# Scores and the carried-state product of a chunked retention kernel as pairs of 64x64 array tiles, in place of zero-padded 128x128 operands

## The chip, the cores and the metric

The kernel runs on one core of one Trainium2 chip. The metric is the device time of one execution in microseconds (us); the profiled span is 1 to 2 us shorter than that time. PE is TensorE's matmul row in the profile and PEld its weight loads; DVE is VectorE, ACT is ScalarE, POOL is GpSimd.

## The reference, cut to what matters

```python
# q, k, v: [8 batches, 8 heads, 576 tokens, 64]; gamma by head; pos = token index
scores = (q @ k.T) / sqrt(64)                        # per batch and head
ret    = scores * where(rel >= 0, gamma ** rel, 0)   # rel = pos_query - pos_key
attn   = ret @ v
x      = attn as [8*576 tokens, 8*64 features]
h      = x @ w_in                                    # 512 -> 2048
out    = maximum(0.01 * h, h) @ w_out                # 2048 -> 512
```

The kernel splits the sequence into chunks of 64 tokens. Inside a chunk it computes masked scores times v; what earlier chunks contribute comes from a carried 64x64 state per head. Two heads are stacked on the 128 partitions (`NP` = 4 such pairs), and a *unit* is up to two chunks (128 tokens) of one batch: 40 units, of which 8 have one chunk only. The two dense layers then run in token blocks, and the attention of later units is threaded between their matmuls.

## The kernel before

Two heads share the 128 rows of the array, and their products must not mix. So the stationary operand is made block diagonal: a 128x128 tile, zeroed once, of which only the two diagonal 64x64 blocks are rewritten. Three tiles of that sort matter: `kdiag` (scores), `sdiag` (carried product) and `vdiag` (product inside the chunk). Writing the two diagonal blocks takes two half-height writes.

```python
# st_transpose(u): tr is PSUM, [P, (q,k), NP, P]
nc.scalar.copy(out=qT[:, :, 0:n], in_=tr[:, 0, :, 0:n])
for hh in range(2):
    eng = nc.scalar.copy if (hh == 0 or u < 2) else nc.vector.tensor_copy
    eng(out=kdiags[z][CH*hh : CH*hh+CH, :, 0:nb, CH*hh : CH*hh+CH], in_=tr[CH*hh : CH*hh+CH, 1, ...])
# st_state(u, j): ut accumulates k^T v in PSUM over three chunks
nc.tensor.matmul(out=ut[:, p, :], lhsT=kstks[z][:, p, j, :], rhs=vst[u][:, p, j, :], ...)
for hh in range(2):
    dst = sd[lo:hi, :, lo:hi]                         # sd is an sdiag
    ...                                               # copy of the state, or ut + sins, by DVE (one of the first by ACT)
# st_scores(u): per p and chunk j
nc.tensor.matmul(out=sc[:, p, j, :], lhsT=kdiags[z][:, p, j, :], rhs=qTs[u][:, p, CH*j : CH*j+CH], ...)
# st_out(u): per chunk j and p, alternating
nc.tensor.matmul(out=o, lhsT=vdiags[z][:, p, j, :], rhs=s16s[u][:, p, j, :], start=True, stop=(i == 0))
if i > 0:
    nc.tensor.matmul(out=o, lhsT=sdiag_at[b, i][:, p, :], rhs=qTs[u][:, p, CH*j : CH*j+CH], start=False, stop=True)
...   # (cuts: loads, casts, dense layers, schedule)
```

Of the kernel before, what the change touches and what calls it, by code (L numbers as in the profile page):

```python
# [11 lines left out]
F16 = mybir.dt.float16  # L12
MUL = mybir.AluOpType.mult
ADD = mybir.AluOpType.add
# [4 lines left out]
def kernel(  # L19
# [16 lines left out]
    nc = tc.nc  # L36
# [3 lines left out]
    P = 128  # L40
    CH = 64
    BLK = 3 * CH
    NP = H // 2
# [9 lines left out]
    for w in range(3):  # L53
        r = ((P * w + np.arange(P)) % BLK)[:, None] - BLK / 2
# [12 lines left out]
    const_pool = ctx.enter_context(tc.tile_pool(name="const", bufs=1))  # L67
    ld_pool = ctx.enter_context(tc.tile_pool(name="ld", bufs=4))
    a_pool = ctx.enter_context(tc.tile_pool(name="ap", bufs=4))
# [22 lines left out]
    w_out16 = const_pool.tile([P, NF, DM], F16, name="w_out16")  # L92

    NZ = 2
    kdiags = [const_pool.tile([P, NP, 2, P], F16, name=f"kdiag{z}") for z in range(NZ)]
    kstks = [const_pool.tile([P, NP, 2, P], F16, name=f"kstk{z}") for z in range(NZ)]
    vdiags = [const_pool.tile([P, NP, 2, P], F16, name=f"vdiag{z}") for z in range(NZ)]
    NS = 3
    sdiags = [const_pool.tile([P, NP, P], F16, name=f"sdiag{z}") for z in range(NS)]
    halves = [const_pool.tile([P, H, D], F16, name=f"half{x}") for x in range(2)]  # L100

    units = [(b, w) for b in range(B) for w in range((S + P - 1) // P)]
# [52 lines left out]
        nc.scalar.copy(out=t[:, :, 0:nb, :], in_=v32[u][:, :, 0:nb, :])  # L155

    qTs = {}
    s16s = {}
    ups = {}
    sins = {}  # L160
    scount = [0]
    sdiag_at = {}

    def st_transpose(u):
        b, w = units[u]
        n = nrows[u]
        nb = n // CH
        z = u % NZ
        for hh in range(2):
            nc.vector.tensor_copy(  # L170
                out=vdiags[z][CH * hh : CH * hh + CH, :, 0:nb, CH * hh : CH * hh + CH],
                in_=vst[u][CH * hh : CH * hh + CH, :, 0:nb, :],
            )
        k16 = qk16[u, 1].rearrange("s (p h) d -> s p h d", h=2)
        if not (w == 4):
            for j in range(nb):
                for hh in range(2):
                    (nc.scalar.copy if u < 4 else nc.gpsimd.tensor_copy)(  # L178
                        out=kstks[z][CH * hh : CH * hh + CH, :, j, CH * hh : CH * hh + CH],
                        in_=k16[CH * j : CH * j + CH, :, hh, :],  # L180
                    )
        tr = tr_pool.tile([P, 2, NP, P], F16, name="tr")
        for x in range(2):
            for p in range(NP):
                nc.tensor.transpose(  # L185
                    tr[:, x, p, :],
                    qk16[u, x][:, 2 * p : 2 * p + 2, :].rearrange("t h d -> t (h d)"),
                    ident,
                )
        qT = a_pool.tile([P, NP, P], F16, name="qT")  # L190
        qTs[u] = qT
        nc.scalar.copy(out=qT[:, :, 0:n], in_=tr[:, 0, :, 0:n])  # L192
        for hh in range(2):
            eng = nc.scalar.copy if (hh == 0 or u < 2) else nc.vector.tensor_copy
            eng(  # L195
                out=kdiags[z][CH * hh : CH * hh + CH, :, 0:nb, CH * hh : CH * hh + CH],
                in_=tr[CH * hh : CH * hh + CH, 1, :, 0:n].rearrange(
                    "e p (j c) -> e p j c", c=CH
                ),
            )  # L200

    def st_state(u, j):
        b, w = units[u]
        z = u % NZ
        i = 2 * w + j
        if i == NI - 1:
            return
        if i % 3 == 0:
            ups[b] = u_pool.tile([P, NP, CH], FP, name="ups")
        ut = ups[b]  # L210
        for p in range(NP):
            nc.tensor.matmul(  # L212
                out=ut[:, p, :],
                lhsT=kstks[z][:, p, j, :],
                rhs=vst[u][:, p, j, :],
                start=(i % 3 == 0 and p == 0),
                stop=(i % 3 == 2),
                skip_group_check=True,
            )
        nxt = i + 1  # L220
        sd = sdiags[scount[0] % NS]
        scount[0] += 1
        sdiag_at[b, nxt] = sd
        if nxt % 3 == 0:
            new = a_pool.tile([P, NP, CH], FP, name="sinit")
            gb = gblk_sb.unsqueeze(2).to_broadcast([P, NP, CH])
            if nxt == 3:
                nc.vector.tensor_tensor(out=new, in0=ut, in1=gb, op=MUL)
            else:
                tmp = a_pool.tile([P, NP, CH], FP, name="stmp")  # L230
                nc.vector.tensor_tensor(out=tmp, in0=ut, in1=sins[b], op=ADD)
                nc.vector.tensor_tensor(out=new, in0=tmp, in1=gb, op=MUL)
            sins[b] = new
        for hh in range(2):
            lo, hi = CH * hh, CH * hh + CH
            dst = sd[lo:hi, :, lo:hi]
            if nxt % 3 == 0:
                nc.vector.tensor_copy(out=dst, in_=sins[b][lo:hi])
            elif nxt < 3:
                (nc.scalar.copy if hh == 0 else nc.vector.tensor_copy)(out=dst, in_=ut[lo:hi])  # L240
            else:
                nc.vector.tensor_tensor(out=dst, in0=ut[lo:hi], in1=sins[b][lo:hi], op=ADD)  # L242

    def st_scores(u):
        b, w = units[u]
        nb = nrows[u] // CH
        z = u % NZ
        sc = sc_pool.tile([P, NP, 2, CH], FP, name="sc")
        for p in range(NP):
            for j in range(nb):  # L250
                nc.tensor.matmul(  # L251
                    out=sc[:, p, j, :],
                    lhsT=kdiags[z][:, p, j, :],
                    rhs=qTs[u][:, p, CH * j : CH * j + CH],
                    start=True,
                    stop=True,
                )
        s16 = a_pool.tile([P, NP, 2, CH], F16, name="s16")
        s16s[u] = s16
        mb = mask_sb.unsqueeze(1)  # L260
        if nb == 2:
            nc.vector.tensor_tensor(  # L262
                out=s16.rearrange("s p j t -> s (p j) t"),
                in0=sc.rearrange("s p j t -> s (p j) t"),
                in1=mb.to_broadcast([P, NP * 2, CH]),
                op=MUL,
            )
        else:
            nc.vector.tensor_tensor(
                out=s16[:, :, 0, :], in0=sc[:, :, 0, :],  # L270
                in1=mb.to_broadcast([P, NP, CH]), op=MUL,
            )

    def st_out(u):
        b, w = units[u]
        n = nrows[u]
        nb = n // CH
        z = u % NZ
        ot = ot_pool.tile([P, NP, P], FP, name="ot")
        for j in range(nb):  # L280
            i = 2 * w + j
            for p in range(NP):
                o = ot[:, p, CH * j : CH * j + CH]
                nc.tensor.matmul(  # L284
                    out=o, lhsT=vdiags[z][:, p, j, :], rhs=s16s[u][:, p, j, :],
                    start=True, stop=(i == 0),
                )
                if i > 0:
                    nc.tensor.matmul(  # L289
                        out=o, lhsT=sdiag_at[b, i][:, p, :],  # L290
                        rhs=qTs[u][:, p, CH * j : CH * j + CH],
                        start=False, stop=True,
                    )
        t0 = b * S + P * w
        nc.scalar.copy(out=xT[:, :, t0 : t0 + n], in_=ot[:, :, 0:n])  # L295

    def prepare(u):
        if u == 4:
            cast(4)
        if u + 4 < NU:  # L300
            load_qk(u + 4)
        if 4 <= u + 3 < NU:
            load_v(u + 3)
        st_transpose(u)
        if u + 1 < NU and u != 3:
            cast(u + 1)

    def slots(u):


        if u == 0:
            yield lambda: prepare(0)
        yield lambda: st_state(u, 0)
        yield lambda: st_scores(u)
        if u + 1 < NU:
            yield lambda: prepare(u + 1)
        if nrows[u] == P:
            yield lambda: st_state(u, 1)
        yield lambda: st_out(u)


    for z in range(NZ):
        nc.vector.memset(kdiags[z], 0.0)
        nc.vector.memset(kstks[z], 0.0)
        nc.vector.memset(vdiags[z], 0.0)
    for z in range(NS):
        nc.vector.memset(sdiags[z], 0.0)
    for x in range(2):
        nc.vector.memset(halves[x], 0.0)
    for u in range(4):  # L330
# [4 lines left out]
    for c in range(4):  # L335
        nc.gpsimd.dma_start(
            out=w_in16[:, :, c * FQ : (c + 1) * FQ],
            in_=moe_w_in[:, c * FQ : (c + 1) * FQ].rearrange("(c k) f -> k c f", k=P),
        )
    for c in range(4):  # L340
        nc.gpsimd.dma_start(
            out=w_out16[:, 4 * c : 4 * c + 4, :],
            in_=moe_w_out[c * FQ : (c + 1) * FQ, :].rearrange("(c k) f -> k c f", k=P),
# [7 lines left out]
    for u in range(NU):  # L351
        b, w = units[u]
        lo = b * S + P * w
# [119 lines left out]
```

## Time and profile before

| | value | where it is read |
|---|---|---|
| time | 354.29 us (354.19 to 354.39, 2 runs) | timed runs |
| profiled span | 353.1 us | page |
| PE busy | 309.0 us (88%) | page, busy table |
| DVE, ACT busy | 176.6 us, 173.1 us | page, busy table |
| PE waits between 62 and 144 us | 6.6 us, all but 1.2 us of it on DVE | waits of PE |
| PE idle from 144 us to its last matmul | none | slices, waits of PE |

These are lines of the page of the kernel before: the busy table, and the span in 40 equal slices of 8.8 us, each digit the busy tenths of a slice.

```profile
span 353.1 us, 7062 instructions
PE 309.0 (88%) x2752; PEld 186.2 (53%) x2752; DVE 176.6 (50%) x383; ACT 173.1 (49%) x340; POOL 97.7 (28%) x172
PE   1336429988988998999999999999999999999995
DMA  7999986365748686534557555555562001101011
```

There are three parts. In the first six slices the loads run at seven to nine tenths and PE waits for its first data. Then comes a middle part, to about 144 us, in which PE is nearly but not quite full. After that PE never idles: there the time is what the PE instructions take.

The waits of PE in the middle part, from 62 to 144 us (who waited <- for whom: us in total, times, longest):

```profile
PE ups L212 <- DVE sdiag L242: 2.3, 2, 1.3
PE ups L212 <- DVE stmp L231: 1.4, 1, 1.4
PE ups L212 <- POOL kstk L178: 1.2, 1, 1.2
PE ups L212 <- DVE sdiag L240: 1.1, 2, 0.6
PE ot L284 <- DVE s L262: 0.6, 1, 0.6
```

6.0 of these 6.6 us are the state matmul (`ups`), and 4.8 of them are spent until DVE has read the PSUM tile that `ups` adds to next.

Last, PE's timeline in the full part (start in us, duration, instruction, count of merged ones). Durations overlap because matmuls are pipelined; the *starts* give the cost.

```profile
182.63 0.28 PE L212 MATMUL ups<-vst,kstk 128*128 128x64 f16 x4
182.75 1.03 PE L405 MATMUL yps<-w_out,gt 128*128 128x512 f16 x4
183.61 0.40 PE L251 MATMUL sc<-qT,kdiag 128*128 128x64 f16 x8
183.85 1.03 PE L382 MATMUL hps<-xT,w_in 128*128 128x512 f16 x4
...
187.00 0.19 PE L284 MATMUL ot<-s,vdiag 128*128 128x64 f16 x1
187.03 0.19 PE L289 MATMUL ot<-qT,sdiag 128*128 128x64 f16 x1
...
187.47 1.03 PE L405 MATMUL yps<-w_out,gt 128*128 128x512 f16 x4
```

Eight padded score matmuls take 0.24 us from their first start to the next instruction, sixteen of the output 0.47 us: 29 ns each, with a new 128x128 weight load each time. Four dense matmuls of 512 columns take 0.86 us.

### The profile page before, as it was taken

The numbers are of one execution on the slowest core, as the hardware profiler recorded it, in microseconds if no ns is written. First come the engines' busy times: TensorE is split into PE (matmuls) and PEld (weight loads), VectorE is DVE, ScalarE is ACT, GpSimd is POOL, SyncE is SP. The second block draws the span as 40 slices with busy tenths as digits, with TensorE's granted clock in tenths as the row PEclk, the third lists the DMA queues.
The fourth block names the chain that finished last, engine by engine and source line by source line (L and its number), as shares of the span: only waits on it lengthen the run. The fifth ranks groups of instructions, "written<-read, shape, count | busy, mean of one in ns | idle before, by whom it ended". The sixth has DMA issues, their size and how long they took to land.

```text
span 353.1 us, 7062 instructions
## 1 busy us (share of the span) xinstructions
PE 309.0 (88%) x2752; PEld 186.2 (53%) x2752; DVE 176.6 (50%) x383; ACT 173.1 (49%) x340; POOL 97.7 (28%) x172
## 2 busy tenths in 40 slices
PE   1336429988988998999999999999999999999995
PEld 0225428546865555555555555555555545566662
DVE  6434420587588588535474746354756344231011
ACT  0955345534764666465546554565547344332320
POOL 9621120251254254143403540232424120000000
PEclk9999968999999999999999999999999999999999
DMA  7999986365748686534557555555562001101011
GB/s 157 205 196 196 208 168 147 72 150 136 153 95 195 148 191 134 121 91 105 121 119 165 123 150 125 130 130 124 126 161 74 32 30 38 54 32 59 32 45 73
DMA packets 116081, 42.46 MB, mean 120 GB/s; under 512 B 106832, under 2 KB 110928, under 8 KB 116048
## 3 DMA queue, kind: packets, MB, share of 16 engines
q1 hardware_dynamic: 111040, 35.67, 43.9%
q0 software_dynamic: 4864, 6.29, 9.8%
q8 instruction: 21, 0.34, 0.4%
q14 instruction: 12, 0.10, 0.1%
q10 hardware_dynamic: 144, 0.06, 0.1%
HBM read 36.76 MB, written 9.44 MB: 131 GB/s over the span
## 4 chain that ended last, share of the span: by engine, by line
PE 74%; DMA 9%; DVE 5%; SPq 4%; ACT 3%; issue 3%; POOL 2%; ACTq 0%; POOLq 0%; DVEq 0%
PE hps L382 33%; PE yps L405 31%; DMA v<-in_v_dram 7%; PE tr L185 4%; SPq L128 3%; PE sc L251 2%; PE ups L212 2%; PE ot L284 2%; PE ot L289 1%; DVE qk L147 1%; SPq L116 1%; POOL kstk L178 1%; DVE osb L415 1%; DMA qk<-in_q_dram 1%; DMA qk<-in_k_dram 1%
## 5 line engine op out<-in xcount | busy, mean ns | idle before, releaser
L382 PE MATMUL hps<-xT,w_in 128*128 128x256 f16 (+1 forms) x768 | 150.1, 333 | 10.1 <-ACT gt L389 7.0
L389 ACT ACTIVATE gt<-hps 128x512 f16<-128x512 f32 x144 | 86.0, 597 | 121.4 <-PE hps L382 120.8
L405 PE MATMUL yps<-w_out,gt 128*128 128x512 f16 x576 | 144.1, 379 | 0.1
L382 PEld LDWEIGHTS <-w_in 128*128 128x128 f16 x768 | 72.3, 100 | 51.7 <-issue 10.4
L178 POOL COPY kstk<-qk 64x256 f16<-64x256 f16 x112 | 44.4, 397 | 161.3 <-DVE qk L147 100.9
L405 PEld LDWEIGHTS <-gt 128*128 128x128 f16 x576 | 51.9, 98 | 47.7 <-issue 0.4
L415 DVE COPY osb<-yps 128x512 f32<-128x512 f32 x36 | 24.7, 690 | 56.9 <-PE yps L405 56.5
L242 DVE TENSOR_TENSOR sdiag<-ups,sinit 64x256 f16<-64x256 f32 x64 | 27.0, 422 | 15.1 <-PE ups L212 14.0
L147 POOL TENSOR_TENSOR qk<-qk,cs 128x512 f16<-128x512 f32 x30 | 31.3, 1046 | 11.1 <-DMA qk<-in_q_dram 9.4
L195 DVE COPY kdiag<-tr 64x512 f16<-64x512 f16 (+1 forms) x38 | 15.2, 400 | 37.4 <-ACT kdiag L195 35.6
L212 PE MATMUL ups<-vst,kstk 128*128 128x64 f16 x256 | 18.5, 196 | 17.2 <-ACT xT L295 8.5
L212 PEld LDWEIGHTS <-kstk 128*128 128x128 f16 x256 | 16.2, 100 | 29.1 <-issue 16.4
L170 DVE COPY vdiag<-vst 64x512 f16<-64x512 f16 (+1 forms) x80 | 26.7, 334 | 8.7 <-ACT vst L155 7.9
L155 ACT CAST vst<-v 128x512 f16<-128x512 f32 (+1 forms) x40 | 23.1, 578 | 15.2 <-DMA v<-in_v_dram 15.2
L192 ACT COPY qT<-tr 128x512 f16<-128x512 f16 (+1 forms) x40 | 21.6, 540 | 15.3 <-PE tr L185 15.0
L185 PE MATMUL tr<-ident,qk 128*128 128x128 f16 x256 | 21.0, 227 | 7.6 <-DVE qk L147 7.6
L262 DVE TENSOR_TENSOR s<-sc,cs 128x512 f16<-128x512 f32 x32 | 22.1, 691 | 6.7 <-PE sc L251 6.1
L295 ACT CAST xT<-ot 128x512 f16<-128x512 f32 (+1 forms) x40 | 21.5, 539 | 7.2 <-PE ot L289 7.2
L147 DVE TENSOR_TENSOR qk<-qk,cs 128x512 f16<-128x512 f32 x34 | 23.4, 692 | 2.2 <-DMA qk<-in_k_dram 0.8
L185 PEld LDWEIGHTS <-qk 128*128 128x128 f16 x256 | 17.5, 102 | 13.3 <-DVE qk L147 7.8
L284 PE MATMUL ot<-s,vdiag 128*128 128x64 f16 x288 | 21.9, 196 | 1.3 <-DVE s L262 1.3
L195 ACT COPY kdiag<-tr 64x512 f16<-64x512 f16 (+1 forms) x42 | 22.7, 540 | 0.1
(34 smaller groups left out, 174.5 us busy)
## 6 DMA issues: line engine op xcount, KB each, us to landing
v<-in_v_dram SPq DMA_DIRECT2D x144, 64.0 KB, 2.9
out_dram<-osb SPq DMA_DIRECT2D x36, 256.0 KB, 2.2
qk<-in_q_dram SPq DMA_DIRECT2D x28, 256.0 KB, 3.6
qk<-in_k_dram SPq DMA_DIRECT2D x28, 256.0 KB, 4.4
w_in<-in_moe_w_in_dram POOLq DMA_DIRECT2D x4, 512.0 KB, 14.8
w_out<-in_moe_w_out_dram POOLq DMA_DIRECT2D x4, 512.0 KB, 23.7
qk<-in_q_dram POOLq DMA_DIRECT2D x4, 256.0 KB, 6.4
qk<-in_k_dram POOLq DMA_DIRECT2D x4, 256.0 KB, 7.4
```

Of the source, the lines that this page charges most:

```text
L147: eng.tensor_tensor(out=t[0:n], in0=qk32[u, x][0:n], in1=tab_sb[0:n, w % 3, x, :].unsqueeze(2).to_broadcast([n, H, D]), op=MUL,)
L170: nc.vector.tensor_copy(out=vdiags[z][CH * hh : CH * hh + CH, :, 0:nb, CH * hh : CH * hh + CH], in_=vst[u][CH * hh : CH * hh + CH, :, 0:nb ...
L178: (nc.scalar.copy if u < 4 else nc.gpsimd.tensor_copy)(out=kstks[z][CH * hh : CH * hh + CH, :, j, CH * hh : CH * hh + CH], in_=k16[CH * j ...
L185: nc.tensor.transpose(tr[:, x, p, :], qk16[u, x][:, 2 * p : 2 * p + 2, :].rearrange("t h d -> t (h d)"), ident,)
L195: eng(out=kdiags[z][CH * hh : CH * hh + CH, :, 0:nb, CH * hh : CH * hh + CH], in_=tr[CH * hh : CH * hh + CH, 1, :, 0:n].rearrange("e p (j ...
L212: nc.tensor.matmul(out=ut[:, p, :], lhsT=kstks[z][:, p, j, :], rhs=vst[u][:, p, j, :], start=(i % 3 == 0 and p == 0), stop=(i % 3 == 2), s ...
L242: nc.vector.tensor_tensor(out=dst, in0=ut[lo:hi], in1=sins[b][lo:hi], op=ADD)
L284: nc.tensor.matmul(out=o, lhsT=vdiags[z][:, p, j, :], rhs=s16s[u][:, p, j, :], start=True, stop=(i == 0),)
L382: nc.tensor.matmul(out=hps[:, f, :], lhsT=w_in16[:, c, fc * P : (fc + 1) * P], rhs=xT[:, c, t0 : t0 + tok], start=(c == 0), stop=(c == NP ...
L389: nc.scalar.activation(out=g_tiles[g][:, fb * nf : (fb + 1) * nf, :], in_=hps, func=mybir.ActivationFunctionType.Lrelu,)
L405: nc.tensor.matmul(out=y_cur[g, tb], lhsT=g_tiles[g][:, f, tb * P : (tb + 1) * P], rhs=w_out16[:, f, :], start=(f == 0), stop=(f == NF - 1),)
L415: nc.vector.tensor_copy(out=osb, in_=y_cur[g, tb])
```

## The change

The intent: give each head its own 64x64 quarter of the array. Head 0 uses rows and columns 0 to 63, head 1 uses 64 to 127; the two are meant to run at once. Then the stationary operand needs no zeros, `kT` is one full-height copy, and the state is one full-height write.

```diff
-        for hh in range(2):
-            eng = nc.scalar.copy if (hh == 0 or u < 2) else nc.vector.tensor_copy
-            eng(out=kdiags[z][CH * hh : CH * hh + CH, ...], in_=tr[CH * hh : CH * hh + CH, 1, ...])
+        kT = a_pool.tile([P, NP, P], F16, name="kT")
+        nc.scalar.copy(out=kT[:, :, 0:n], in_=tr[:, 1, :, 0:n])
 ... st_state
-        for hh in range(2):  (two half-height writes into sdiag)
+        one full-height write: sd = a_pool.tile([P, NP, CH], F16, name="s_st")
 ... st_scores
-                nc.tensor.matmul(out=sc[:, p, j, :], lhsT=kdiags[z][:, p, j, :], rhs=qTs[u][:, p, CH*j : CH*j+CH], ...)
+                for hh in range(2):
+                    r = slice(CH * hh, CH * hh + CH)
+                    nc.tensor.matmul(out=sc[r, p, j, :], lhsT=kTs[u][r, p, CH*j : CH*j+CH],
+                                     rhs=qTs[u][r, p, CH*j : CH*j+CH], ...)
 ... st_out: first all vdiag products of the unit (128x128, as before), then, in a loop of their own,
+            for p in range(NP):
+                for hh in range(2):
+                    r = slice(CH * hh, CH * hh + CH)
+                    nc.tensor.matmul(out=ot[r, p, c], lhsT=sdiag_at[b, i][r, p, :], rhs=qTs[u][r, p, c],
+                                     start=False, stop=True, ...)
 ... the memsets of kdiag and sdiag go
```

More of the change, by code (lines that the diff above doesn't have):

```diff
@@ L94 @@
     NZ = 2
-    kdiags = [const_pool.tile([P, NP, 2, P], F16, name=f"kdiag{z}") for z in range(NZ)]
     kstks = [const_pool.tile([P, NP, 2, P], F16, name=f"kstk{z}") for z in range(NZ)]
     vdiags = [const_pool.tile([P, NP, 2, P], F16, name=f"vdiag{z}") for z in range(NZ)]
-    NS = 3
-    sdiags = [const_pool.tile([P, NP, P], F16, name=f"sdiag{z}") for z in range(NS)]
     halves = [const_pool.tile([P, H, D], F16, name=f"half{x}") for x in range(2)]
@@ L157 @@
     qTs = {}
+    kTs = {}
     s16s = {}
@@ L160 @@
     sins = {}
-    scount = [0]
     sdiag_at = {}
@@ L192, in st_transpose @@
         nc.scalar.copy(out=qT[:, :, 0:n], in_=tr[:, 0, :, 0:n])
-        for hh in range(2):
-            eng = nc.scalar.copy if (hh == 0 or u < 2) else nc.vector.tensor_copy
-            eng(
-                out=kdiags[z][CH * hh : CH * hh + CH, :, 0:nb, CH * hh : CH * hh + CH],
-                in_=tr[CH * hh : CH * hh + CH, 1, :, 0:n].rearrange(
-                    "e p (j c) -> e p j c", c=CH
-                ),
-            )
+        kT = a_pool.tile([P, NP, P], F16, name="kT")
+        kTs[u] = kT
+        nc.scalar.copy(out=kT[:, :, 0:n], in_=tr[:, 1, :, 0:n])
     def st_state(u, j):
@@ L220, in st_state @@
         nxt = i + 1
-        sd = sdiags[scount[0] % NS]
-        scount[0] += 1
+        sd = a_pool.tile([P, NP, CH], F16, name="s_st")
         sdiag_at[b, nxt] = sd
@@ L233, in st_state @@
             sins[b] = new
-        for hh in range(2):
-            lo, hi = CH * hh, CH * hh + CH
-            dst = sd[lo:hi, :, lo:hi]
-            if nxt % 3 == 0:
-                nc.vector.tensor_copy(out=dst, in_=sins[b][lo:hi])
-            elif nxt < 3:
-                (nc.scalar.copy if hh == 0 else nc.vector.tensor_copy)(out=dst, in_=ut[lo:hi])
-            else:
-                nc.vector.tensor_tensor(out=dst, in0=ut[lo:hi], in1=sins[b][lo:hi], op=ADD)
+        if nxt % 3 == 0:
+            nc.vector.tensor_copy(out=sd, in_=sins[b])
+        elif nxt < 3:
+            nc.vector.tensor_copy(out=sd, in_=ut)
+        else:
+            nc.vector.tensor_tensor(out=sd, in0=ut, in1=sins[b], op=ADD)
     def st_scores(u):
@@ L250, in st_scores @@
             for j in range(nb):
-                nc.tensor.matmul(
-                    out=sc[:, p, j, :],
-                    lhsT=kdiags[z][:, p, j, :],
-                    rhs=qTs[u][:, p, CH * j : CH * j + CH],
-                    start=True,
-                    stop=True,
-                )
+                for hh in range(2):
+                    r = slice(CH * hh, CH * hh + CH)
+                    nc.tensor.matmul(
+                        out=sc[r, p, j, :],
+                        lhsT=kTs[u][r, p, CH * j : CH * j + CH],
+                        rhs=qTs[u][r, p, CH * j : CH * j + CH],
+                        start=True,
+                        stop=True,
+                    )
         s16 = a_pool.tile([P, NP, 2, CH], F16, name="s16")
@@ L281, in st_out @@
             i = 2 * w + j
+            c = slice(CH * j, CH * j + CH)
             for p in range(NP):
-                o = ot[:, p, CH * j : CH * j + CH]
                 nc.tensor.matmul(
-                    out=o, lhsT=vdiags[z][:, p, j, :], rhs=s16s[u][:, p, j, :],
-                    start=True, stop=(i == 0),
-                )
-                if i > 0:
+                    out=ot[:, p, c], lhsT=vdiags[z][:, p, j, :], rhs=s16s[u][:, p, j, :],
+                    start=(j == 0 and p == 0), stop=(i == 0), skip_group_check=True,
+                )
+        for j in range(nb):
+            i = 2 * w + j
+            c = slice(CH * j, CH * j + CH)
+            if i == 0:
+                continue
+            for p in range(NP):
+                for hh in range(2):
+                    r = slice(CH * hh, CH * hh + CH)
                     nc.tensor.matmul(
-                        out=o, lhsT=sdiag_at[b, i][:, p, :],
-                        rhs=qTs[u][:, p, CH * j : CH * j + CH],
-                        start=False, stop=True,
+                        out=ot[r, p, c], lhsT=sdiag_at[b, i][r, p, :],
+                        rhs=qTs[u][r, p, c], start=False, stop=True,
+                        skip_group_check=True,
                     )
@@ L322 @@
     for z in range(NZ):
-        nc.vector.memset(kdiags[z], 0.0)
         nc.vector.memset(kstks[z], 0.0)
         nc.vector.memset(vdiags[z], 0.0)
-    for z in range(NS):
-        nc.vector.memset(sdiags[z], 0.0)
     for x in range(2):
```

## The prediction

> **What bounds the kernel now.** TensorE is busy 309.0 of 353.1 us (page, busy table) and the chain of waits that ended last is 74% PE. By stretches: from 0 to 50 us the loads decide (DMA share about 1.2 from 10 to 40 us; PE busy only 3 to 7 us in each 10). From 63 to 125 us PE is some 90% busy; waits on DVE, ACT and POOL results there come to only about 6 us (waits of PE). From 126 us to the end PE never idles: that stretch is worth what the PE instructions cost. 61% of the score matmuls and 64% of the carried-state ones run there.
>
> In that stretch eight score matmuls take 0.24 us start to start (timeline: 183.61 to 183.85), and the alternating vdiag/sdiag pairs start every 0.029 us (180.44, 180.47, 180.50). So a 128x128 weight load plus 64 columns costs 29 ns; a whole unit of 8 scores plus 8 carried products costs only about 0.47 us.
>
> **What the change removes.** DVE: kdiag copies 38 x 400 ns = 15 us, and one of two half-height state writes (64 x 422 ns = 27 us, so about 13 us); and 2 us of early memsets. ACT: kdiag 22.7 us and 6 us of state casts against one full kT copy, 40 x 540 = 21.6 us. DVE (176.6 us) and ACT (173.1 us) are at half load, so after 126 us this buys nothing; before it, I give it 3 us (shorter ACT/DVE sequences between transposes, scores and state).
>
> **What it adds on PE.** 288 scores become 576 instructions, 256 carried products become 512. The two of a pair can overlap at best, so a pair can hardly beat 29 ns. The Trainium skill, "TensorEngine Tiling (Array Packing)", says in Key Properties that changing the tiling mode drains the array, and under Restrictions that column tiling disables fast weight load. This trace has no tiled instruction, so it shows neither.
> - Pairs: my estimate is 60 ns a pair (two instructions at the measured 29 ns cadence), 31 ns more. 544 pairs: 17 us; about 340 pairs after 126 us: 10.5 us.
> - Mode switches: in and out of the scores, in and out of the carried batch, which now follows all vdiag products: 4 a unit, about 98 after 126 us. A lone 64-column matmul takes 0.19 us in the trace against 0.03 us of cadence, so an undrained pipe hides up to 0.16 us. Estimate 0.07 us a switch: 7 us there.
> - Before 126 us PE is partly idle: +2 us.
>
> Sum: 10.5 + 7 + 2 - 3 = +16.5 us. **Predicted 370 us, range 355 to 395. Faster by over 2%: 0.08; within 2%: 0.27; slower by over 2%: 0.65.**
>
> **What would show each step.** Right: the timeline after 126 us shows score and carried bursts of 16 taking clearly over 0.24 us (about 0.5), with a gap before and after that the old bursts lack; PE stays without idle after about 126 us; the stretch before 126 us ends no later than 2 us from now. DVE busy falls by some 28 us, ACT by some 7 us, without shortening the span.
>
> **What would make it wrong.** If both tiles load and stream fully in parallel (pair at 30 ns) and switches cost little, the result lies within 2%. If loads without the fast mode serialise (over 100 ns a pair) or each drain exposes the whole 0.16 us and the next load, it goes towards 395 us or beyond. Faster needs the first 126 us to be limited by DVE/ACT far more than the waits show, or a pair well under 29 ns.

## More of the kernel before

Now one line of the waits of DVE over the whole span:

```profile
DVE kdiag L195 <- ACT kdiag L195: 35.6, 29, 3.0
```

DVE stands still ahead of its half of `kdiag` until ACT has written the other half. Only 4.5 of these 35.6 us lie between 62 and 144 us; 28.3 lie after it, where PE never waits. But what is queued behind on DVE stands too. One instance, in the timelines of DVE and (last line) PE:

```profile
127.02 0.43 DVE L195 COPY kdiag<-tr 64x512 f16<-64x512 f16 x1 [0.52 <-ACT kdiag L195]
127.48 0.69 DVE L147 TENSOR_TENSOR qk<-qk,cs 128x512 f16<-128x512 f32 x1
128.20 0.69 DVE L415 COPY osb<-yps 128x512 f32<-128x512 f32 x1
128.92 0.43 DVE L240 CAST sdiag<-ups 64x256 f16<-64x256 f32 x1
129.40 0.28 PE L212 MATMUL ups<-vst,kstk 128*128 128x64 f16 x4 [0.49 <-DVE sdiag L240]
```

The `ups` matmuls that feed this state read had ended at 126.83 us; DVE came to the read 2.1 us later, behind the wait for ACT (0.52 us), the `kdiag` copy and two other pieces of work, and PE stood for 0.49 us.

## The result, and the profile after

The changed kernel took 363.06 us (362.98 to 363.14, 2 runs) against 354.29 us: 8.8 us more. The ratio is 1.0248, with a 95% interval of 1.0203 to 1.0292. Ratios in this document are the mean time of one kernel's fast runs over that of the other's of the same rounds, so not quite the ratio of the medians that are quoted. A kernel is called slower or faster here when the whole interval lies on one side of 1; whether a difference is over 2% is another question, and for `half_writes` and `kact_spool` below the interval leaves it open. The result was correct.

Lines of the page of the changed kernel, to be held against those of before:

```profile
span 361.2 us, 8042 instructions
PE 325.7 (90%) x3296; PEld 192.7 (53%) x3296; DVE 135.0 (37%) x292; ACT 170.0 (47%) x322; POOL 97.5 (27%) x172
PE   0426549999999999999999999999999999999995
```

DVE lost 41.6 us of work, and the eights of the PE row are gone: PE has no wait at all after 62 us. Yet the kernel is slower. One stretch shows both sides of it, the middle part from 62 to 144 us (length, busy us and instruction counts of each engine, granted clock, DMA share, GB/s). The kernel before:

```profile
62.00:144.00 82.00, 75.33 (x821) 49.41 (x819) 59.97 (x126) 46.81 (x97) 32.02 (x58) 1.00 0.61 138
```

and the changed one:

```profile
62.00:144.00 82.00, 82.00 (x1028) 52.61 (x1026) 44.71 (x100) 46.15 (x90) 31.93 (x58) 1.00 0.64 145
```

PE went from 75.3 to 82.0 busy us in 82. The next table gives the times of three landmarks, taken from the traces: the start of the 16th and of the 49th activation of the dense layer (of 144), and the end.

```
                  16th at   16th to 49th   49th to end
before             62.3 us     81.5 us       209.2 us
changed            61.2 us     80.2 us       219.7 us
```

The changed kernel is level or ahead until 144 us and loses 10.5 us after it, where PE was full already. (The 1.1 us at the 16th is no merit of the change: PE idles for some 7 us before 50 us in both, and its granted clock is then halved for 10.2 us in the one trace and 6.8 us in the other; other runs of both sorts show either.) What it loses is in PE's timeline of the changed kernel:

```profile
187.24 0.40 PE L274 MATMUL ot<-s,vdiag 128*128 128x64 f16 x8
187.57 0.44 PE L286 MATMUL ot<-qT,s_st 64*64 64x64 f16 x16
187.94 1.04 PE L399 MATMUL yps<-w_out,gt 128*128 128x512 f16 x4
...
189.68 1.03 PE L399 MATMUL yps<-w_out,gt 128*128 128x512 f16 x4
190.63 0.31 PE L241 MATMUL sc<-qT,kT 64*64 64x64 f16 x8
190.88 1.04 PE L376 MATMUL hps<-xT,w_in 128*128 128x512 f16 x4
```

Sixteen tiled matmuls (eight pairs) take 0.37 us from first start to the next instruction, eight of them (four pairs) 0.25 us. So four more pairs cost 0.12 to 0.13 us, about 32 ns a pair, hardly more than the 29 ns of one padded matmul; and about 0.12 us is there whatever the count. The single starts in the trace say it more exactly. The second of a pair starts 3 to 4 ns after the first and the next pair 28 to 29 ns later, so a pair takes 31.7 ns. Only the step from the first pair to the second is wider, by 20 ns, once in each burst whatever its length (a *burst* is an unbroken run of tiled matmuls). And the first tiled matmul starts 123 ns after the last padded one where 29 ns was usual, and 309 ns after a 512-column matmul where 216 ns was usual: 94 ns going in. The first 128x128 one starts 125 ns after the last tiled one: some 96 ns going out. The four dense matmuls ahead of the scores take 0.95 us (189.68 to 190.63) instead of 0.86 us.

The weight loads of the same stretch show what is lost at the seam:

```profile
187.03 0.49 PEld L274 LDWEIGHTS <-vdiag 128*128 128x128 f16 x8
187.57 0.33 PEld L286 LDWEIGHTS <-s_st 64*64 64x64 f16 x16
187.94 0.55 PEld L399 LDWEIGHTS <-gt 128*128 128x128 f16 x4
188.60 0.74 PEld L376 LDWEIGHTS <-w_in 128*128 128x128 f16 x4
```

Between instructions of one mode the load runs ahead: `vdiag` is loaded from 187.03 for a matmul at 187.24, `w_in` from 188.60 for one at 188.81. At both seams, 187.57 and 187.94, load and matmul start together: nothing was loaded ahead. That fits the Trainium skill, "TensorEngine Tiling (Array Packing)", Key Properties, which states that changing the tiling mode drains the array; it gives no time for it. Whether the draining or the missing load ahead makes the cost, no run here separates.

One burst in and out of the 64x64 mode thus costs about 0.21 us (94 + 96 + 20 ns), plus 2.7 ns a pair. The trace counts 80 bursts, 72 of them after 62 us and 484 pairs in these: 72 x 0.21 + 484 x 0.0027 = 16.4 us. Less the 6.6 us of waits that went away, that is +9.8 us; 8.8 us were measured.

### The profile page after: what moved, and what is told of

Its sections match the earlier page's. It is cut to its first block, busy times and chain, and to the rows that moved or that the text cites. A ratio compares the mean times of both kernels' runs of the same rounds, so it can differ in the third digit from the quotient of the medians.

```text
span 361.2 us, 8042 instructions
## 1 busy us (share of the span) xinstructions
PE 325.7 (90%) x3296; PEld 192.7 (53%) x3296; DVE 135.0 (37%) x292; ACT 170.0 (47%) x322; POOL 97.5 (27%) x172
## 4 chain that ended last, share of the span: by engine, by line
PE 86%; DMA 7%; SPq 4%; ACT 2%; issue 0%; DVE 0%; ACTq 0%
PE hps L376 36%; PE yps L399 35%; DMA v<-in_v_dram 7%; PE tr L182 4%; PE sc L241 4%; PE ot L286 3%; SPq L125 3%; PE ot L274 2%; PE ups L204 2%; SPq L113 1%; ACT kstk L175 0%; ACT vst L152 0%; ACT gt L383 0%; DVE osb L409 0%; ACT qT L189 0%
## 5 line engine op out<-in xcount | busy, mean ns | idle before, releaser
L376 PEld LDWEIGHTS <-w_in 128*128 128x128 f16 x768 | 71.4, 100 | 56.1 <-issue 13.4
L167 DVE COPY vdiag<-vst 64x512 f16<-64x512 f16 (+1 forms) x80 | 23.3, 291 | 13.8 <-ACT vst L152 13.0
L230 DVE TENSOR_TENSOR s_st<-ups,sinit 128x256 f16<-128x256 f32 x32 | 13.5, 423 | 32.9 <-PE ups L204 32.9
L192 ACT COPY kT<-tr 128x512 f16<-128x512 f16 (+1 forms) x40 | 22.0, 550 | 0.0
L241 PEld LDWEIGHTS <-kT 64*64 64x64 f16 x576 | 12.6, 112 | 15.7 <-issue 8.5
L241 PE MATMUL sc<-qT,kT 64*64 64x64 f16 x576 | 17.1, 199 | 2.2 <-ACT kT L192 2.2
```

Of the source, the lines that this page charges most:

```text
L167: nc.vector.tensor_copy(out=vdiags[z][CH * hh : CH * hh + CH, :, 0:nb, CH * hh : CH * hh + CH], in_=vst[u][CH * hh : CH * hh + CH, :, 0:nb ...
L241: nc.tensor.matmul(out=sc[r, p, j, :], lhsT=kTs[u][r, p, CH * j : CH * j + CH], rhs=qTs[u][r, p, CH * j : CH * j + CH], start=True, stop=True,
L376: nc.tensor.matmul(out=hps[:, f, :], lhsT=w_in16[:, c, fc * P : (fc + 1) * P], rhs=xT[:, c, t0 : t0 + tok], start=(c == 0), stop=(c == NP ...
```

## The experiments

Two theories were at stake for the loss. The *drain theory*: each change between the modes costs, whatever runs within. The *pair theory*, that of the prediction: two instructions for one cost. And one question for the gain: what in the removed work freed PE of its waits?

**1. Either half alone.** In `scores_only` only the scores are tiled, in `carried_only` only the carried product; the other part is word for word that of the kernel before.

```diff
 scores_only:   kdiag -> kT and tiled st_scores; sdiag and st_out as before
 carried_only:  sdiag -> s_st and tiled carried loop; kdiag and st_scores as before
```

> Only the scores are tiled (one burst of 64x64 a unit), the carried product stays padded. Drain theory (0.22 us for each burst in and out of the 64x64 mode, read from the changed kernel's timeline; 36 units after 62 us, where PE has no slack): +8 us, minus about 3 us of relief from the DVE copies of kdiag: about 359 us, half of the whole loss. Pair theory (each tile pair costs more than the padded matmul): the same sign, but the burst of 16 would take well over 0.47 us. If the loss sits in the carried product alone: 351 to 354 us.

> Only the carried product is tiled, scores stay on the padded kdiag. Drain theory: +8 us for 36 bursts, minus about 3 us of relief from the single state write: about 359 us. If the loss came from the scores alone: 351 to 354 us. If costs add, the changes of the two half versions against the kernel before add up to that of the full change (+8.8 us), within 2 us.

`scores_only` took 356.46 us (ratio 1.007, 1.0048 to 1.0093) and `carried_only` 359.14 us (1.015, 1.0129 to 1.017), the kernel before 353.84 us. So +2.6 and +5.3 us, together +7.9 us against +8.8 us of the whole. Each half costs; they add up within 2 us. I had expected them to be equal, and they are not. But the trace gives both the same burst of 16 at 0.37 us, and from the 49th activation to the end both take the same 214.5 us, 5.3 us more than the kernel before: the two halves of the 10.5 us of the whole. All of the difference lies earlier. From the 16th to the 49th activation `carried_only` takes 81.0 us and `scores_only` 79.4 us, and the PE waits that remain there are 2.8 us against 1.6 us. The 16th comes at 62.4 us against 60.9 us; in the profiled executions the granted clock was halved for 10.2 us and 6.8 us.

**2. The relief without the tiling.** `half_writes` gives a wrong result: it is the kernel before with one of the two half-height writes left out.

```diff
-        for hh in range(2):            # kdiag
+        for hh in range(1):
-        for hh in range(2):            # sdiag
+        for hh in range(1, 2):
```

> Wrong result on purpose: the kernel before, padded tiles and all its PE work, but only one of the two half-height writes of kdiag and of the state tile, so that DVE and ACT do as much as in the changed kernel. It measures the relief without the tiling. My reading of the waits (6.5 us of PE waits between 62 us and 175 us that the changed kernel lost): about 348 us. Rival (relief is worth nothing or 3 us at most, as the prediction had it): 351 to 354 us, and then the drains must cost less than the 0.22 us a burst that I read.

It took 346.25 us, ratio 0.9779 (0.9755 to 0.9804). The stretch from 62 to 144 us, PE first:

```profile
62.00:144.00 82.00, 81.08 (x878) 52.79 (x875) 49.34 (x102) 49.10 (x97) 34.55 (x63) 1.00 0.65 149
```

The removed copies were worth 7.6 us, more than twice the 3 us of the prediction. From the 16th to the 49th activation it takes 74.9 us instead of 81.5 us, and from there to the end the same 209.2 us: the relief lies where PE waited. So the tiling itself costs about 363.06 - 346.25 = 16.8 us, and 7.6 us of that, nearly half, came back through the copies that it makes needless. (About, because the relief is not quite the same: DVE is busy for 142.5 us in `half_writes` and 135.0 us in the changed kernel, ACT for 167.6 and 170.0 us.)

**3. Half of the changes of mode.** `merged` issues the scores of the next unit right behind the carried products of this one.

```diff
+    def out_scores(u):
+        st_out(u)
+        if u + 1 < NU:
+            st_scores(u + 1)
```

> The changed kernel with the scores of the next unit issued right behind the carried products of this one: as many tile pairs, but one burst a unit and so half of the mode changes. Drain theory: 36 x 0.215 = 7.7 us less than the changed kernel, about 355 us. Pair theory (the instructions cost, not the changes): no gain, 362 to 364 us.

It took 356.74 us (1.0085, 1.0063 to 1.0107), 6.3 us less than the changed kernel, with the same tile pairs in 41 bursts instead of 80. Its timeline:

```profile
204.29 0.40 PE L274 MATMUL ot<-s,vdiag 128*128 128x64 f16 x8
204.62 0.44 PE L286 MATMUL ot<-qT,s_st 64*64 64x64 f16 x16
204.90 0.42 PE L241 MATMUL sc<-qT,kT 64*64 64x64 f16 x16
205.25 1.04 PE L382 MATMUL hps<-xT,w_in 128*128 128x512 f16 x4
```

Where more tiled matmuls follow, the first sixteen take 0.28 us instead of 0.37 us: no way out and no way in.

**4. Many more changes of mode.** `alternating` is the changed kernel with each carried pair behind its own `vdiag` product.

```diff
         for j in range(nb):
             for p in range(NP):
                 nc.tensor.matmul(out=ot[:, p, c], lhsT=vdiags[...], ...)
-        for j in range(nb):   # a loop of its own
-            for p in range(NP):
-                for hh in range(2):
+                for hh in range(2):        # if i > 0
                     nc.tensor.matmul(out=ot[r, p, c], lhsT=sdiag_at[b, i][r, p, :], ...)
```

> The changed kernel with each carried pair right behind its own vdiag product, in the order of the kernel before, so up to 8 changes into the 64x64 mode a unit where there was one. Same instructions, same data. Drain theory: 7 more bursts for a full unit at 0.215 us, about 54 us over the units after 62 us: 410 to 420 us. Pair theory (cost is in the instructions): 363 us as the changed kernel.

It took 405.36 us in its one run (of unknown state, since it ran once; its granted clock was 0.99, as in fast runs), and the result was correct. Its timeline:

```profile
200.65 0.19 PE L274 MATMUL ot<-s,vdiag 128*128 128x64 f16 x1
200.78 0.22 PE L282 MATMUL ot<-qT,s_st 64*64 64x64 f16 x2
200.92 0.20 PE L274 MATMUL ot<-s,vdiag 128*128 128x64 f16 x1
201.06 0.22 PE L282 MATMUL ot<-qT,s_st 64*64 64x64 f16 x2
```

Every step is 0.13 to 0.15 us, though it holds one matmul or one pair. My 410 to 420 us was too high because I had counted seven extra bursts for every unit; the trace counts 296 bursts against 80, 216 more, and 42.3 us / 216 = 0.196 us each. But 24 of these 216 fall before the 16th activation, where the loads decide. The fair measure is the part in which PE is always full, from the 49th activation to the end; `out_tiled` is experiment 5:

```
49th to end              time     bursts   pairs
before, half_writes     209.2 us     0        0
scores_only             214.5 us    22      156
carried_only            214.5 us    22      140
merged                  214.6 us    22      288
changed                 219.7 us    44      296
out_tiled               220.1 us    44      452
alternating             245.8 us   162      296
```

From changed to `alternating` 118 bursts more cost 26.1 us, 0.22 us each, at the same number of pairs; from changed to `out_tiled` 156 pairs more cost 0.4 us, 2.4 ns each. These two figures give all six tiled kernels within 0.3 us. So `merged` saved there 5.1 us, about what 22 bursts cost (4.9 us). Before that it is no faster than the changed kernel: in its profiled execution the scores waited for `kT` for 11.2 us in five waits, nearly all of it before 62 us, and the granted clock was halved for 13.7 us.

**5. More pairs, no more changes.** `out_tiled` tiles the product inside the chunk too, straight from the stacked v, in the same burst as the carried product.

```diff
-                    out=ot[:, p, c], lhsT=vdiags[z][:, p, j, :], rhs=s16s[u][:, p, j, :],
+                    out=ot[r, p, c], lhsT=vst[u][r, p, j, :], rhs=s16s[u][r, p, j, :],    # hh = 0, 1
 (vdiag, its copies and memsets go)
```

> The changed kernel with the intra-chunk product tiled too, straight from the stacked v: no vdiag tile and no vdiag copies (23 us less on DVE), 288 padded matmuls become 576 of 64x64 within the same burst, so no mode change more. Drain theory: 363 us, within 2 us: pairs at 31 ns cost 2 ns more than the padded 29 ns, and the relief is already used up. Pair theory of the prediction (31 ns more a pair): 8 us more, about 371 us.

It took 363.35 us (1.027, 1.0243 to 1.0297), 0.3 us from the changed kernel, with 288 pairs more and 80 bursts as before. Its timeline:

```profile
187.20 0.44 PE L270 MATMUL ot<-s,vst 64*64 64x64 f16 x16
187.48 0.42 PE L282 MATMUL ot<-qT,s_st 64*64 64x64 f16 x16
187.83 1.04 PE L394 MATMUL yps<-w_out,gt 128*128 128x512 f16 x4
```

Thirty-two tiled matmuls take 0.63 us where the changed kernel took 0.70 us for eight padded and sixteen tiled; the way in, which there lay between the two, now lies ahead of the first (the four `hps` matmuls before it take 0.95 us). The pair theory (371 us) falls. It shows as well that the relief is used up: the `vdiag` copies went from DVE too, and nothing came of it.

**6. Which work of DVE held PE up?** `pool_v1` and `pool_v2` are the kernel before, untiled, with one or both `vdiag` half copies on POOL from the fifth unit on.

```diff
-            nc.vector.tensor_copy(out=vdiags[z]...
+            (nc.gpsimd if hh == 1 and u >= 4 else nc.vector).tensor_copy(...   # pool_v1; pool_v2: both hh
```

> The kernel before, padded and untiled, with one of the two vdiag half copies of each unit from the fifth on moved from DVE to POOL (about 12 us less on DVE, of 176). If the relief of DVE is what helps the part before 126 us: some 3 us of the 7.6 us that the half writes gave, about 350 to 351 us. If it was ACT or the early memsets: 354 us.

> As pool_v1 with both vdiag half copies on POOL (about 24 us less on DVE). If DVE relief helps and POOL is not too slow: 348 to 350 us. If POOL becomes the late one (it already makes kstk and scales q): waits of PE on POOL appear and it is slower than pool_v1.

Both missed: 354.18 us (1.0003, 0.9981 to 1.0025) and 353.83 us (0.9992, 0.9972 to 1.0011) against 353.92 us. Busy time of DVE fell from 176.6 to 160.0 us in `pool_v2` (16.6 us, not the 24 us that I had reckoned with), and PE gained nothing: from 62 to 144 us it waited 6.1 us on DVE, against 5.4 us before. So it is not DVE's load as such. Three lines of the waits of PE in `pool_v1` from 62 to 144 us are nearly those of before (the third is POOL again, now at `vdiag`):

```profile
PE ups L212 <- DVE sdiag L242: 2.0, 2, 1.0
PE ups L212 <- DVE stmp L231: 1.5, 1, 1.5
PE ups L212 <- POOL vdiag L170: 1.5, 2, 0.9
```

**7. The order of the DVE queue.** `kdiag_act` puts both halves of `kdiag` on ACT; `s_pool` lets DVE write the state once, full height, and POOL copy it into the padded tile; `kact_spool` does both. All are untiled and correct.

```diff
 kdiag_act
-            eng = nc.scalar.copy if (hh == 0 or u < 2) else nc.vector.tensor_copy
+            nc.scalar.copy(out=kdiags[z]...)
 s_pool, from the fifth unit on
+            st = a_pool.tile([P, NP, CH], F16, name="s_st")      # one DVE write, full height
+            for hh in range(2):
+                nc.gpsimd.tensor_copy(out=sd[lo:hi, :, lo:hi], in_=st[lo:hi])
```

> The kernel before, untiled, with both half copies of kdiag on ACT for every unit (38 copies, 15 us, off the DVE queue; 20 us more on ACT, which is half idle). In the kernel before DVE stands idle 35.6 us ahead of these copies, waiting for ACT's half, and everything behind it in the DVE queue waits too. Theory A (the relief came from this head-of-line wait): the PE waits on DVE between 62 and 144 us shrink from 6.7 us to 3 or less, about 350 us. Theory B (it came from the second state write alone, or from DVE load as such, which the POOL versions already speak against): 353 to 354 us.

> The kernel before, untiled, with one full-height state write on DVE (as in the changed kernel) and the two half copies into the padded tile on POOL, from SBUF, from the fifth unit on. Theory A: the kdiag wait in the DVE queue stays, so little: 352 to 354 us. Theory B: the wait of the state matmul for the state reads shrinks, about 350 us.

> Both of these together: all of the relief, correct, and without a 64x64 mode. If A and B each hold a part: 347 to 349 us, close to the half writes (346.25 us) and faster than both kernels by about 1.5 to 2% against the kernel before.

Against 354.16 us of the kernel before they took 352.28 us (0.995, 0.9916 to 0.9984), 353.01 us (0.9965, 0.9933 to 0.9997) and 347.65 us (0.9818, 0.9774 to 0.9862). Each alone gave 1 to 2 us, less than the 4 us that either theory claimed for itself; the two together gave 6.5 us. So it is neither alone: with one of them left in the DVE queue PE still waits for the state reads. The stretch from 62 to 144 us (PE, PEld, DVE, ACT, POOL) of `pool_v2`:

```profile
62.00:144.00 82.00, 75.01 (x824) 49.19 (x822) 52.96 (x100) 46.73 (x95) 51.51 (x86) 1.00 0.60 139
```

of `kdiag_act`:

```profile
62.00:144.00 82.00, 77.79 (x843) 50.72 (x841) 52.96 (x117) 56.86 (x112) 32.72 (x60) 1.00 0.64 146
```

and of `kact_spool`:

```profile
62.00:144.00 82.00, 81.08 (x878) 52.95 (x877) 51.77 (x101) 58.49 (x112) 55.69 (x109) 1.00 0.66 150
```

DVE is equally busy in the first two (52.96 us), and 1.2 us less in the third, but PE gets 75.0, 77.8 and 81.1 us of work done. So it is not how much DVE does that counts. What fits all runs is the time that DVE stands waiting for ACT in its queue, because two tiles, `kdiag` and the first two `sdiag` of a batch, are written half by ACT and half by DVE. The waits from 62 to 144 us:

```
                DVE waits for ACT's half    PE waits
before            5.3 us                     6.6 us
pool_v2          13.8 us                     6.8 us
kdiag_act        10.8 us (all at sdiag)      4.0 us
s_pool            9.3 us (all at kdiag)      5.9 us
half_writes       0                          1.0 us
kact_spool        0                          0.9 us
```

In `pool_v2` DVE, freed of work, only stood longer at `kdiag` (13.0 us against 4.5 us). In `kdiag_act` and `s_pool` the wait that was taken away came back at the other shared tile. Only where neither tile is shared did PE fill up. (The cause is inferred from these runs together: each of them also moves some work, and none changes the sharing alone.) The PE waits of `kact_spool` in that stretch come to 0.9 us; the largest is

```profile
PE ups L211 <- DVE s_st L240: 0.3, 1, 0.3
```

`kact_spool` is faster than both kernels: by 6.5 us (1.8%) than the one before, and by 15.4 us than the changed one by the medians of different rounds.

## Why the prediction was right or wrong

The time was inside the range (355 to 395 us), the sign was right and so was the frame: PE is full after the middle part, the tile pairs save it nothing, and the changes of mode land there. But +16.5 us was nearly twice the +8.8 us measured. The largest term of the sum, the pairs, was hardly there at all; the other costs and the relief were too small, and these errors cancel in part. With the pairs alone put right the same sum would have been +6.9 us, or 1.9%: that the kernel came out slower by over 2%, as forecast, is partly luck.

- *"Pairs: my estimate is 60 ns a pair"*: 31.7 ns, 2.7 ns more than the padded matmul and not 31. For the 332 pairs after 126 us that is 0.9 us, not 10.5 us. I had given each instruction of a pair its own 29 ns step; the two run at once and start 3 to 4 ns apart. The Trainium skill, "TensorE: Matmul & The Clock Gate", Part 3, states this for packed matmuls ("Δstart ≈ 4ns", drawn for tiles of 32 rows); I had not used it. `out_tiled` settles the point: 288 more pairs, +0.3 us. This is the step that failed.
- *"Estimate 0.07 us a switch: 7 us there"*: about 0.105 us, the wider step shared out. The trace has 49 bursts after 126 us, so 98 switches as counted: 10.3 us. The count was right and the size too low by a third.
- *"Before 126 us PE is partly idle: +2 us"* and *"before it, I give it 3 us"* of relief: the relief is 6.6 us by the waits and 7.6 us by `half_writes`; 23 bursts before 126 us and after 62 us cost about 5 us with their pairs. I had read that waits of "only about 6 us" were there, and then credited half of them. They all went.
- With the measured terms: 0.9 + 10.3 + 5 - 6.6 = +9.6 us, or +8.6 us with the 7.6 us of `half_writes`.
- The signs named: the burst of 16 did take over 0.24 us, but 0.37 us and not 0.5; the seams before and after it were there; PE stayed full; the early part did not end later. DVE fell by 41.6 us instead of 28 us: I had left out the state copies of L238 (11.0 us before, 5.0 us after), and the remaining `vdiag` copies became shorter (291 ns on the mean, 334 ns before). ACT fell by 3 us instead of 7 us, which I did not follow up.
- The prediction named the end of the fast weight load under column tiling as a cost (the Trainium skill, "TensorEngine Tiling (Array Packing)", Restrictions). No run here shows a cost: a pair of 64x64 loads and matmuls starts every 32 ns.

## What to carry to other kernels

Small array tiles replaced a padded 128x128 operand at nearly the same rate here (32 ns a pair against 29 ns), but each burst of them cost 0.21 to 0.22 us of a full PE; so count the changes, not the instructions, and gather tiled work into few long bursts before you tile. Measure what a change removes apart from what it adds, with a deliberately wrong kernel if need be: here the copies alone were worth 7.6 us, and 6.5 us of that was to be had without the tiling. And a half-idle engine can hold up the critical one: look at what stands in its queue ahead of the piece that others wait for, since taking 17 us of other work off DVE gave nothing, while ending the two waits for ACT's half of a shared tile (with DVE 23 us less busy) gave 6.5 us.

## What the Trainium skill lacked or had wrong

- "TensorEngine Tiling (Array Packing)", Key Properties, says that changing the mode drains the array but not what that costs. Here, between 128x128 and 64x64: 94 ns going in (123 ns from start to start instead of 29, or 309 instead of 216) and about 96 ns going out, with no weight load run ahead at either seam, and 20 ns once inside the burst; 0.22 us a burst from the times of `alternating` and the changed kernel where PE is full.
- The same page, Restrictions, lists the loss of the fast weight load under column tiling. It cannot be seen: pairs of 64x64 tiles, each with new weights, start every 32 ns, against 29 ns for a 128x128 load and 64 columns.
- The same page, Gotcha 1, says that different row tiles cannot access the same PSUM bank simultaneously. Here the two tiles of each pair use different row groups and write the two partition halves of one bank, 3 to 4 ns apart; the results were correct and the cadence was not broken. So the sentence on this page, as it stands, is too wide for tiles that differ in column group too.
- "TensorE: Matmul & The Clock Gate", Part 3, was right on the 4 ns between the tiles of a pack: 3 to 4 ns here.
- No page that I read names the head-of-line effect (work that waits behind a stalled piece in the same queue): here DVE stood 35.6 us, 4.5 us of them in the middle part, ahead of its half of a tile whose other half ACT was writing. Taking it away gave 1.9 us alone, since the wait came back at the next tile shared with ACT, and 6.5 us when both were gone.
